# Score tiles leave PSUM in two instructions instead of three: one over 768 columns in two banks, one over 384

## The chip, the cores and the metric

The kernel runs on one core of a Trainium2 chip. The metric is the device time of one execution in microseconds, from the median of several runs. A core has TensorE (PE in the profile; its weight loads are PEld), VectorE (DVE), ScalarE (ACT), GpSimd (POOL) and SyncE (SP). TensorE writes its results to PSUM, which this kernel uses as eight banks of 512 fp32 columns on 128 partitions; VectorE and ScalarE carry them from there to SBUF.

## The reference

```python
# attention: batch 4, 8 heads, 1152 keys, head_dim 64; neighbouring queries are averaged: 576 queries
q_pool = q.reshape(B, H, S // 2, 2, D).mean(axis=3)
scores = scale * np.matmul(q_pool, k.transpose(0, 1, 3, 2))
scores = scores - np.max(scores, axis=-1, keepdims=True)
attn = np.exp(scores)
attn = attn / (np.sum(attn, axis=-1, keepdims=True) + 1e-09)
attn_out = np.matmul(attn, v)
...
# then, on x of (4, 576, 512):
mixed = np.real(fft(fft(x, axis=1), axis=2))
u = x + mixed
un = (u - mean(u)) / np.sqrt(var(u) + 1e-06)
out = u + np.maximum(un @ w_ch1, 0.0) @ w_ch2      # w_ch1 512 x 2048, w_ch2 2048 x 512, kept as float64
```

## The kernel before

The 32 heads are worked in 16 pairs. A pair has five units: for query blocks 0 to 3 a unit holds two score tiles, one of each head of the pair, of 128 queries by 1152 keys; the last unit holds one tile in which the last 64 queries of both heads are stacked. While the tiles of one unit are turned and multiplied by the values, the scores of the next unit are computed, so each pass of the loop in `attention` issues on TensorE, in this order: score pieces of the next unit, the product with the values of the unit before (`av`, L263), groups of transposes of this unit (`t_step`, L247), with more score pieces between the groups.

A score tile is made in three pieces of 384 columns (`s_piece`, L220 and L222). Each piece is two accumulating matmuls into one bank (four in the stacked tile), and one VectorE instruction that scales it, stores it to SBUF (`sp`) and keeps the smallest value of each row in a column of `bia`; the second and third piece take the column of the piece before as an operand, so the last column holds the smallest value of the row. The eviction is recorded as two instructions, the pass itself and a short read of the accumulator. When all pieces of a tile are out, ScalarE takes the exponential over the 1152 columns in place (`s_exp`, L234). In the next pass the tile is turned, four blocks of 128 columns to a group, and each group is copied from PSUM to `pt`, by ScalarE except for the fourth group of a two-tile unit, which VectorE copies (L250).

Below, the two tiles of a unit are A and B, their pieces A0, A1, A2, B0, B1, B2, and the five groups of transposes g0 to g3 (four blocks each) and gc (the last block of both tiles). A pass of the kernel before then runs on TensorE: A0, A1, `av`, g0, A2, B0, g1, B1, B2, g2, g3, gc. A mark as in A0' means the same step in the next pass.

PSUM is split into three pools: `ps_t`, five banks, for all score pieces and most transposes; `ps_o`, one, for `av`; `ps_f`, two, for the dense layers. While the first four pairs run, no dense layer runs yet, and four of five groups of transposes go to `ps_f` (by a counter, `steps`). A pool hands out its banks in turn, so an allocation waits until what was written to the same bank as many allocations ago as the pool has banks has been read out.

Between the steps of a pass the generator yields an estimate of its TensorE time, and a planner (`background`, `credit`, `due`) puts in the other work: blocks of the dense layers (`ffn`, twelve matmuls into one bank, L685 to L687, then ScalarE L704 and VectorE L705, or VectorE L717), the Fourier transform and the normalisation of a finished batch (`dft`, `norm`, mostly chains of VectorE instructions), the conversion of the weights from float64 (`convert`, ScalarE, VectorE and GpSimd), and the reciprocal of the row sums (`den_recip`: VectorE L271 and L272, then a transpose on TensorE at L276). Instructions on each engine run in the order in which they are written out this way. After the last unit (`tail`) the dense layers of the last batches use all banks of `ps_t` and `ps_f`, chosen by the counter `turn`.

## Time and profile before

| | |
|---|---|
| median of 3 runs | 1044.74 us (1042.09 to 1045.94) |
| the profiled execution: its own time | 1044.25 us |
| its span, first to last instruction | 1042.5 us |
| mean granted TensorE clock over the span | 0.981 |
| TensorE busy | 975.8 us, 94% of the span |
| VectorE busy | 605.4 us, 58% |
| ScalarE busy | 523.7 us, 50% |
| score evictions on VectorE (L222) | 432, of 384 columns each |

The span is 1.75 us shorter than the execution's own time. Busy time of TensorE counts pipelined matmuls until their modelled end, so where it is 100% the engine is without a gap, but not at its peak. The clock is a share of 2.4 GHz: 0.5 would be 1.2 GHz throughout. A row of waits names who stood idle, behind the arrow what ended the idle time, then the total, how often, and the longest.

### The profile page before, as it was taken

How to read it: one execution, taken by the hardware profiler on the slowest of the kernel's cores; microseconds unless marked ns; L12 is line 12 of the kernel's file. 1: busy time of each engine (PE TensorE's matmuls, PEld its weight loads, DVE VectorE, ACT ScalarE, POOL GpSimd, SP SyncE). 2: the span in 40 equal slices, each digit the busy share in tenths (PEclk: the TensorE clock that was granted, in tenths of full speed). 3: DMA queues.
4: the chain of work that ended last, by engine and by line, in shares of the span. 5: the costliest groups of instructions: out<-in, count | busy, mean ns of one | idle time of the engine just before them, and what ended most of it. 6: DMA issues, size and time to landing. Idle time of an engine off the chain costs nothing.

```text
span 1042.5 us, 19731 instructions
## 1 busy us (share of the span) xinstructions
PE 975.8 (94%) x7392; PEld 847.5 (81%) x7392; DVE 605.4 (58%) x1518; ACT 523.7 (50%) x1017; POOL 421.7 (40%) x609
## 2 busy tenths in 40 slices
PE   6999988898998899899999999999999989999998
PEld 4898977777877777687788888787788867899998
DVE  5556868889754687787644475666544245522222
ACT  5778877767745566466444554554444231201100
POOL 3555678788386575996323141633200010000000
PEclk9999999999999899999999999999999989999999
DMA  6545467646566856475745464163532334733443
GB/s 186 170 135 180 135 197 239 183 127 221 143 203 243 276 181 220 140 240 187 217 145 179 135 193 129 33 207 109 170 104 102 115 120 126 230 134 122 126 136 122
DMA packets 62515, 170.91 MB, mean 164 GB/s; under 512 B 16770, under 2 KB 20242, under 8 KB 62420
## 3 DMA queue, kind: packets, MB, share of 16 engines
q1 hardware_dynamic: 58100, 151.96, 46.1%
q0 software_dynamic: 4320, 17.70, 5.3%
q8 instruction: 58, 0.95, 0.4%
q14 instruction: 37, 0.30, 0.1%
HBM read 146.88 MB, written 22.75 MB: 163 GB/s over the span
## 4 chain that ended last, share of the span: by engine, by line
PE 50%; DVE 5%; POOL 3%; ACT 2%; DMA 2%; issue 1%; SPq 0%; DVEq 0%; ACTq 0%; POOLq 0%
PE f L685 7%; PE f L687 6%; PE f L686 6%; PE s L220 6%; PE o L263 5%; PE t L247 5%; PE t L685 4%; PE t L687 4%; PE t L686 4%; DVE sp L222 1%; DMA out<-x 1%; PE f L505 1%; DMA w<-w 1%; POOL wb L646 1%; POOL rest L646 0%
## 5 line engine op out<-in xcount | busy, mean ns | idle before, releaser
L222 DVE TENSOR_SCALAR_CACHE_REDUCE sp<-s,bia 128x384 f32<-128x384 f32 x288 | 177.2, 615 | 79.2 <-PE s L220 57.2
L220 PE MATMUL s<-ks,qh 128*128 128x384 f32 x480 | 185.7, 387 | 19.8 <-ACT qh L164 6.4
L234 ACT ACTIVATE sp<-sp,bia 128x1152 f32<-128x1152 f32 x144 | 180.2, 1256 | 1.8 <-DVE sp L222 1.6
L263 PE MATMUL o<-pt,vs 128*64 128x128 f32 (+1 forms) x2880 | 171.7, 273 | 9.4 <-DVE pt L250 5.0
L263 PEld LDWEIGHTS o<-pt,vs 128*64 128x64 f32 x2880 | 151.5, 141 | 33.6 <-issue 20.7
L250 ACT COPY pt<-t 128x512 f32<-128x512 f32 (+2 forms) x243 | 124.5, 527 | 91.3 <-PE t L247 90.2
L220 PE MATMUL s<-ks,ql 128*128 128x384 f32 x480 | 164.9, 344 | 0.4 <-POOL ql L165 0.4
L247 PE MATMUL t<-ident,sp 128*128 128x128 f32 x1045 | 150.6, 276 | 7.1 <-DVE sp L222 3.7
L247 PEld LDWEIGHTS t<-ident,sp 128*128 128x128 f32 x1045 | 121.5, 141 | 28.3 <-DVE sp L222 6.7
L220 PEld LDWEIGHTS s<-ks,qh 128*128 128x128 f32 x480 | 92.4, 193 | 31.7 <-ACT pt L250 9.0
L189 POOL TENSOR_TENSOR ks<-kr,ks 64x288 fp32r<-64x288 f32 x120 | 103.4, 894 | 29.7 <-issue 12.6
L705 DVE SCALAR_TENSOR_TENSOR g<-f,g 128x512 fp32r<-128x512 f32 (+1 forms) x52 | 34.7, 667 | 110.0 <-ACT g L704 110.0
L220 PEld LDWEIGHTS s<-ks,ql 128*128 128x128 f32 x480 | 93.1, 194 | 1.1 <-POOL ql L165 0.8
L704 ACT ACTIVATE g<-f 128x512 fp32r<-128x512 f32 (+1 forms) x52 | 30.1, 579 | 119.7 <-PE f L687 119.7
L186 POOL TENSOR_TENSOR qr<-qr 128x288 f32<-128x288 f32 x60 | 49.9, 850 | 92.6 <-DMA qr<-in_q 92.6
L197 POOL TENSOR_TENSOR ql<-qr,qh 128x288 fp32r<-128x288 f32 (+2 forms) x75 | 55.7, 768 | 75.0 <-ACT qh L194 73.7
L685 PE MATMUL f<-unh,w 128*128 128x512 f32 (+1 forms) x208 | 82.8, 398 | 2.7 <-DMA w<-w 2.7
L646 POOL TENSOR_TENSOR rest<-rest,wa 128x256 f32<-128x256 f32 x64 | 48.2, 770 | 89.2 <-DVE wa L639 64.0
L222 DVE TENSOR_SCALAR_CACHE_REDUCE sp<-s 128x384 f32<-128x384 f32 x144 | 78.4, 545 | 6.1 <-PE s L220 4.4
L687 PE MATMUL f<-unl,w 128*128 128x512 f32 (+1 forms) x208 | 80.4, 387 | 0.0
L686 PE MATMUL f<-unh,w 128*128 128x512 f32 (+1 forms) x208 | 80.2, 386 | 0.0
L685 PE MATMUL f<-g,w 128*128 128x512 f32 (+1 forms) x188 | 74.2, 394 | 1.9 <-DVE g L705 0.9
(149 smaller groups left out, 1761.3 us busy)
## 6 DMA issues: line engine op xcount, KB each, us to landing
w<-w SPq DMA_DIRECT2D x128, 512.0 KB
qr<-in_q SPq DMA_DIRECT2D x30, 576.0 KB
ks<-in_k POOLq DMA_DIRECT2D x30, 576.0 KB, 6.1
wraw<-in_w SPq DMA_DIRECT2D x32, 512.0 KB
w<-wraw SPq DMA_DIRECT2D x32, 512.0 KB
vs<-in_v SPq DMA_DIRECT2D x32, 288.0 KB
kr<-in_k SPq DMA_DIRECT2D x30, 288.0 KB
out<-x SPq DMA_DIRECT2D x12, 256.0 KB
```

The costliest lines, as they stand in the source:

```text
L189: nc.gpsimd.tensor_tensor(ks[D:, c], kr[D:, c], ks[D:, c].bitcast(F32), op=ALU.subtract)
L197: nc.gpsimd.tensor_tensor(ql[:, z], qr[:, 0, x:y], qh[:, z].bitcast(F32), op=ALU.subtract)
L220: nc.tensor.matmul(ps, lhsT=l, rhs=k, start=i == 0, stop=i == len(ops) - 1)
L222: nc.vector.tensor_scalar(sp[n, j][:, c], ps, -0.0625, bt[:, pc - 1:pc] if pc else None, op0=ALU.mult, op1=ALU.min, accum_out=bt[:, pc:pc ...
L234: last_exp[0] = nc.scalar.activation(t, t, AF.Exp, bias=bia.pop((n, j))[:, 2:3], scale=-1.0, accum_out=den[pr][:, col:col + 1]).ins
L247: nc.tensor.transpose(ps[:, i * P:i * P + P], sp[k][:, c * P:(c + 1) * P], ident)
L250: (nc.vector.tensor_copy if eng == "v" else nc.scalar.copy)(pt[:, :o], ps[:, :o])
L263: nc.tensor.matmul(po[y * D:y * D + D, :w], lhsT=qkv[2 * pr + y][3][:, c, :], rhs=pt[:, o:o + w], start=c == 0, stop=c == NKC - 1)
L646: nc.gpsimd.tensor_tensor(o[:, c], x[:, c], y[:, c], op=op)
L685: nc.tensor.matmul(ps, lhsT=ah, rhs=bh, start=first, stop=False)
L686: nc.tensor.matmul(ps, lhsT=al, rhs=bh, start=False, stop=False)
L687: nc.tensor.matmul(ps, lhsT=ah, rhs=bl, start=False, stop=last)
```

## The change

Each score tile leaves PSUM in two instructions. The first two pieces become one: four matmuls (two for each half) into a tile of two neighbouring banks, and one eviction over 2 x 384 columns. The third piece stays as it was, in a bank of `ps_t`. Two of the five banks of `ps_t` become the new pool `ps_s`, which holds one such wide tile; `ps_t` keeps three. Where a pass issued two pieces it now issues one (wide, small, wide, small), and the last small piece stands between g2 and g3. A wide piece is called A0 or B0 from here on and a small one A1 or B1, so a pass is: A0, `av`, g0, A1, g1, B0, g2, B1, g3, gc. In the first four pairs two of five groups of transposes go to `ps_t` instead of one, and in the tail the dense layers turn through five banks instead of seven, since `ps_s` isn't used there.

```diff
--- before.py
+++ after.py
@@ -72,7 +72,8 @@
     xp = pool("x", XB)
     scr = pool("scr", 2, space=bass.MemoryType.DRAM)
     scw = pool("scw", 1, space=bass.MemoryType.DRAM)
-    ps_t = pool("ps_t", 5, space=PSUM)
+    ps_t = pool("ps_t", 3, space=PSUM)
+    ps_s = pool("ps_s", 1, space=PSUM)
     ps_o = pool("ps_o", 1, space=PSUM)
     ps_f = pool("ps_f", 2, space=PSUM)
 
@@ -95,7 +96,7 @@
     def gtile():
 
         turn[0] += 1
-        if tail[0] and turn[0] % 7 < 5:
+        if tail[0] and turn[0] % 5 < 3:
             return ps_t.tile([P, 512], F32, tag="t", name="t")
         return ps_f.tile([P, 512], F32, tag="f", name="f")
 
@@ -209,21 +210,27 @@
     def s_piece(n, j, pc):
         if pc == 0:
             sp[n, j] = spp.tile([P, S], F32, tag="sp", name="sp")
-            bia[n, j] = smp.tile([P, 3], F32, tag="bia", name="bia", bufs=6)
-        ps = ps_t.tile([P, 512], F32, tag="t", name="s")[:, :384]
-        c = slice(pc * 384, pc * 384 + 384)
+            bia[n, j] = smp.tile([P, 2], F32, tag="bia", name="bia", bufs=6)
+        if pc == 0:
+            ps = ps_s.tile([P, 2, 512], F32, tag="s", name="s")[:, :, :384]
+        else:
+            ps = ps_t.tile([P, 1, 512], F32, tag="t", name="s")[:, :, :384]
+        n_c = 2 - pc
         ops = []
         for m in (n, n + 1) if j == 4 else (n,):
             ks, qh, ql, _ = qkv[m]
-            ops += [(t[:, j * P:j * P + P], ks[:, c]) for t in (qh, ql)]
-        for i, (l, k) in enumerate(ops):
-            nc.tensor.matmul(ps, lhsT=l, rhs=k, start=i == 0, stop=i == len(ops) - 1)
+            ops += [(t[:, j * P:j * P + P], ks) for t in (qh, ql)]
+        for x in range(n_c):
+            c = slice((2 * pc + x) * 384, (2 * pc + x) * 384 + 384)
+            for i, (l, k) in enumerate(ops):
+                nc.tensor.matmul(ps[:, x], lhsT=l, rhs=k[:, c], start=i == 0, stop=i == len(ops) - 1)
         bt = bia[n, j]
+        c = slice(pc * 768, pc * 768 + n_c * 384)
         nc.vector.tensor_scalar(
-            sp[n, j][:, c], ps, -0.0625, bt[:, pc - 1:pc] if pc else None,
+            sp[n, j][:, c].rearrange("p (a b) -> p a b", a=n_c), ps, -0.0625, bt[:, 0:1] if pc else None,
             op0=ALU.mult, op1=ALU.min, accum_out=bt[:, pc:pc + 1],
         )
-        return 740 if j == 4 else 390
+        return (740 if j == 4 else 390) * n_c
 
     def s_exp(n, j):
         pr = n // 2
@@ -231,7 +238,7 @@
             den[pr] = smp.tile([P, 9], F32, tag="den", name="den", bufs=3)
         t = sp[n, j]
         col = 5 * (n % 2) + j
-        last_exp[0] = nc.scalar.activation(t, t, AF.Exp, bias=bia.pop((n, j))[:, 2:3], scale=-1.0,
+        last_exp[0] = nc.scalar.activation(t, t, AF.Exp, bias=bia.pop((n, j))[:, 1:2], scale=-1.0,
                                            accum_out=den[pr][:, col:col + 1]).ins
 
     steps = [0]
@@ -239,7 +246,7 @@
     def t_step(pr, items, eng):
 
         steps[0] += 1
-        if pr < 4 and steps[0] % 5 != 2:
+        if pr < 4 and steps[0] % 5 not in (2, 4):
             ps = ps_f.tile([P, 512], F32, tag="f", name="f")
         else:
             ps = ps_t.tile([P, 512], F32, tag="t", name="t")
@@ -329,11 +336,12 @@
         for _ in parts(0):
             pass
         for pc, _ in enumerate(parts(1)):
-            s_piece(0, 0, pc)
+            if pc < 2:
+                s_piece(0, 0, pc)
         for _, q_part, _, _, _ in first:
             q_part(*Q0[1])
         s_exp(0, 0)
-        for pc in range(3):
+        for pc in range(2):
             s_piece(1, 0, pc)
         s_exp(1, 0)
         nc.sync.dma_start(onesm, cst[4, :, P:2 * P])
@@ -354,7 +362,7 @@
                 if j in (1, 3):
                     prep_head(2 * pr + 2 + j // 2)
             nxt = unit_tiles(*units[i + 1]) if i + 1 < len(units) else []
-            pieces = deque((n, jj, pc) for n, jj in nxt for pc in range(3))
+            pieces = deque((n, jj, pc) for n, jj in nxt for pc in range(2))
             expd = []
 
             def some(k):
@@ -363,7 +371,7 @@
                     if pieces:
                         p = pieces.popleft()
                         pe += s_piece(*p)
-                        if p[2] == 2:
+                        if p[2] == 1:
                             expd.append(p[:2])
                 return pe
 
@@ -390,15 +398,17 @@
             else:
                 k = tiles[0]
                 g = [[(k, c, [(0, 0), (1, D)]) for c in cs] for cs in (range(4), range(4, 8), range(8, 9))]
-            yield some(2)
+            yield some(1)
             if held:
                 yield finish(*held)
             yield tr(g[0], "a")
-            yield some(2)
+            yield some(1)
             yield tr(g[1], "a")
-            yield some(2)
+            yield some(1)
             for y, x in enumerate(g[2:]):
                 yield tr(x, "v" if j < 4 and y == 1 else "a")
+                if y == 0:
+                    yield some(1)
             exps()
             if j == 4:
                 after(1500, den_recip(pr))
```

## Rows read from the trace of the kernel before

**Rows 1.** The page's first part: busy time, share of the span, instructions, by engine.
```profile
PE 975.8 (94%) x7392; PEld 847.5 (81%) x7392; DVE 605.4 (58%) x1518; ACT 523.7 (50%) x1017; POOL 421.7 (40%) x609
```

**Rows 2.** Windows by stage: length, busy (xcount) by engine, granted clock, DMA.
```profile
20.00:130.00 110.00, 106.83 (x1118) 96.77 (x1117) 72.07 (x224) 85.98 (x170) 62.10 (x98) 1.00 0.53 160
130.00:520.00 390.00, 351.22 (x2789) 294.83 (x2788) 286.69 (x683) 244.95 (x473) 272.74 (x376) 0.96 0.63 201
520.00:820.00 300.00, 293.77 (x2312) 251.80 (x2310) 155.99 (x407) 147.78 (x288) 74.75 (x111) 1.00 0.42 133
820.00:1042.50 222.50, 212.78 (x1151) 196.53 (x1149) 80.29 (x178) 35.86 (x70) 5.67 (x8) 0.98 0.46 142
```

**Rows 3.** TensorE's waits, 130 to 520 us: total us, times, longest us.
```profile
PE t L276 <- DVE den L272: 5.2, 6, 1.5
PE o L263 <- DVE pt L250: 5.0, 4, 2.8
PE o L263 <- ACT pt L250: 4.1, 2, 3.9
PE s L220 <- DVE sp L222: 3.9, 5, 2.2
PE s L220 <- ACT pt L250: 3.7, 4, 1.7
PE t L247 <- DVE sp L222: 3.3, 3, 2.1
PE t L247 <- ACT pt L250: 3.0, 2, 2.5
...
PE f L247 <- ACT pt L250: 2.5, 2, 2.1
```

**Rows 4.** TensorE's waits, 20 to 130 us: all that is listed.
```profile
PE f L247 <- ACT pt L250: 3.2, 8, 1.2
```

**Rows 5.** VectorE's groups by shape: the evictions of score pieces (busy, mean ns).
```profile
L222 DVE TENSOR_SCALAR_CACHE_REDUCE sp<-s,bia 128x384 f32<-128x384 f32 x288 | 177.2, 615 | 79.2 <-PE s L220 57.2 <-DVE sp L222 0.5
L222 DVE TENSOR_SCALAR_CACHE_REDUCE sp<-s 128x384 f32<-128x384 f32 x144 | 78.4, 545 | 6.1 <-PE s L220 4.4 <-ACT pt L250 1.5
```

**Rows 6.** VectorE's timeline, one unit near 58 us: start, duration.
```profile
58.14 0.55 DVE L222 TENSOR_SCALAR_CACHE_REDUCE sp<-s 128x384 f32<-128x384 f32 x1
...
58.82 0.62 DVE L222 TENSOR_SCALAR_CACHE_REDUCE sp<-s,bia 128x384 f32<-128x384 f32 x1
...
59.57 0.62 DVE L222 TENSOR_SCALAR_CACHE_REDUCE sp<-s,bia 128x384 f32<-128x384 f32 x1
...
60.11 0.68 DVE L250 COPY pt<-t 128x512 f32<-128x512 f32 x1
```

**Rows 7.** TensorE's timeline in the same unit.
```profile
58.10 0.42 PE L220 MATMUL s<-ks,qh 128*128 128x384 f32 x1
...
58.53 0.34 PE L220 MATMUL s<-ks,qh 128*128 128x384 f32 x1
...
58.89 0.60 PE L247 MATMUL f<-ident,sp 128*128 128x128 f32 x4
59.32 0.60 PE L247 MATMUL t<-ident,sp 128*128 128x128 f32 x4
59.76 0.38 PE L247 MATMUL f<-ident,sp 128*128 128x128 f32 x2
59.90 0.42 PE L220 MATMUL s<-ks,qh 128*128 128x384 f32 x1
```

**Rows 8.** ScalarE's timeline in the same unit.
```profile
58.44 0.59 ACT L250 COPY pt<-f 128x512 f32<-128x512 f32 x1 [0.45 <-PE f L247]
59.58 0.97 ACT L250 COPY pt<-f 128x512 f32<-128x512 f32 x2 [0.55 <-PE f L247]
```

**Rows 9.** TensorE's timeline: a wait near 432 us.
```profile
432.52 0.44 PE L220 MATMUL s<-ks,qh 128*128 128x384 f32 x1 [2.22 <-DVE sp L222]
```

**Rows 10.** Windows around a shorter wait near 299 us and that one.
```profile
295.00:310.00 15.00, 13.28 (x99) 11.14 (x97) 10.17 (x23) 8.27 (x18) 14.03 (x21) 1.00 0.49 164
425.00:440.00 15.00, 12.47 (x84) 9.17 (x82) 13.46 (x30) 6.03 (x11) 13.89 (x20) 0.89 0.31 112
```

## The prediction

> **What bounds the kernel now.** I read the busy times first: TensorE is busy 94% of the span, no other engine above 58% except its own weight loads [rows 1]. So what the change takes off VectorE is worth only what TensorE waits for VectorE. Next the windows by stage [rows 2]: TensorE stands idle 3.2 us from 20 to 130 us (the first pairs, no dense layers), 38.8 us from 130 to 520 (390 minus 351.2; conversions, transforms and dense layers run beside the attention), 6.2 us from 520 to 820, and 9.7 us behind that, when no score tile is left. The middle stretch decides. VectorE is busy 73.5% of it (286.7 of 390), 52% of the stretch behind.
>
> The waits of that stretch say what ended the idle time [rows 3]. VectorE ends 17.4 us in 18 waits: 5.2 for the reciprocals, 5.0 for the copy of g3, 3.9 and 3.3 for score evictions that hold a bank. ScalarE's copies to `pt` end 13.3 us (4.1, 3.7, 3.0, 2.5). In the first stretch the whole list is one row: transposes that wait in `ps_f` for ScalarE, 3.2 us [rows 4].
>
> A long wait costs more than itself. The wait of 2.22 us at 432.5 us ended on a score eviction [rows 9]; the windows around it have a granted clock of 0.89, those around a wait of 1.7 us (the longest of that row of [rows 3]) have 1.00 [rows 10]. An 0.11 share of 15 us is 1.65 us of TensorE time lost, as if 3.3 us ran at 1.2 instead of 2.4 GHz. That it was the wait that lowered the clock is a reading from these two, not shown.
>
> **What VectorE saves.** In a clean unit its evictions start 0.68, 0.75 and 0.54 us apart [rows 6]: 1.97 us a tile. Their mean lengths are 545 ns without and 615 ns with the operand from the piece before [rows 5]. The wide eviction is in no row. The copy of 512 columns takes 0.68 [rows 6] and the eviction of 384 takes 0.545, so a column is worth about 1.05 ns, and 384 more columns about 0.40 us: the wide one lasts 0.95, and the next starts 1.08 behind its start (0.68 + 0.40). A tile then holds VectorE for 1.08 + 0.54 = 1.62 us, 0.35 less, a two-tile unit 0.70 less, all 144 tiles 50 us. The bounds: if two banks in one instruction cost as much as two instructions (2 x 0.545 = 1.09 long), 0.21 a tile is left; if the columns are all that counts and a column costs less, 0.40. I take 0.35. The matmuls are as many as before, and so are their loads; ScalarE's work is the same.
>
> **What that is worth on TensorE.** First, the 18 waits on VectorE can shrink by at most 0.70 each, 12.6 us, when each follows a unit whose evictions are queued ahead of it. But some are shorter than 0.70, and a TensorE that comes earlier meets the same chain of the transform or the conversion earlier. I take half, 6.3 us (bounds 0 and 12.6). Second, the banks: a group of transposes waited for an eviction (A2, B0) to free its bank, 3.3 us in three waits. Now transposes take the bank of an earlier transpose, or of a small piece long evicted; this lies within the 6.3. Third, the clock: the two longest waits on score evictions, 2.2 and 2.1 us, would come down to about 1.5, below the 1.7 that left the clock at 1.00. I count 2 x 1.65 = 3.3 us (bounds 0 and 5).
>
> **What the first pairs gain.** Before, g2, g3 and gc often fall to the two banks of `ps_f` in a row, and gc waits for ScalarE's copy of g2. With two of five groups in `ps_t` (steps 2 and 4), gc follows an allocation two or three groups back in each of the four pairs, by the counter's phase. I take 4 of the 5.7 us (3.2 and 2.5) [rows 3, 4]; bounds 1 and 5.7.
>
> **What three banks cost.** From the fifth pair on, `ps_t` serves g0, A1, g1, g2, B1, g3, gc, and each allocation waits for the third before it. For most steps the work between is as long as before. One is new: gc waits for g2, with only B1 and g3 between. In the clean unit g2 starts at 58.89, g3 takes 0.44, a small piece 0.36 (58.53 to 58.89) [rows 7]; so gc wants to start 0.43 + 0.36 + 0.44 = 1.23 us behind g2's start. ScalarE starts the copy of g2 0.69 behind that start (59.58) and copies for 0.59 [rows 8]: 1.28. So gc is 0.05 to 0.1 late in a unit where the planner puts nothing between, when ScalarE is prompt, and as late as ScalarE is when it isn't. The cap is the work that TensorE could have done before `av` needs the same copy: gc 0.14 and A0' some 0.8, about 0.9 us, and what the planner puts between. Twelve pairs with three such units (in the fourth no small piece stands there) are 36. At 0.1 each that is 3.6 us. For the 18 of the crowded stretch I add as much again and a little, 0.12 each, since ScalarE is late there at times (its 13.3 us): 2.2, together 5.8 us (bounds 0 and 36 x 0.9 = 32).
>
> **What the single wide buffer costs.** A0' waits until B0 is evicted. Between are g2 0.43, B1 0.36, g3 0.44, gc 0.14 [rows 7]: 1.37 us. Against it stand 1.08 of VectorE and the way from TensorE to the reader, 0.26 as ScalarE shows it (59.32 to 59.58): 1.34. Any foreign instruction ahead of it on VectorE makes A0' late, and behind A0' stands `av` in TensorE's queue; but before the change VectorE had five pieces to finish by then (3.40 us), now three instructions (2.70). I take 1.5 us in all (bounds 0 and 15). The copy of g3 on VectorE comes behind B1, nearer to `av`, which reads it from its ninth matmul on; that is in the half that I left out above. The planner's estimates per pass add up to the same, `s_exp` and the startup keep their order. In the tail five banks instead of seven turn under blocks of twelve matmuls, at 0.18 us each (212.8 over 1151 [rows 2]) 2.2 us a block. Its eviction is hidden by the four blocks that follow before the bank is used again, 8.9 us, so I cost it at nothing; without that cover the tail would show waits on L704 and L705.
>
> The sum goes against the profiled execution: 1044.25 - 4 - 6.3 - 3.3 + 5.8 + 1.5 = 1037.95, so 1038 us. That execution lies 0.5 below the median of the runs, within their spread of 3.9.
>
> The Trainium skill (Perfetto Trace Analysis, section Optimizing Scalar/DVE Operations) says that larger operations help where the engine is saturated, and that where it isn't, but leaves gaps on others, smaller ones may complete sooner. The 73.5% and 52% here lie below saturation, so by that rule the fourth way below would decide and the sum would be its 1051; by the rows it is 1038. The 17.4 us for which TensorE waits on VectorE [rows 3] are gaps that a late queue left, not a long instruction, and so the rows bear the first half of the rule out rather than the second.
>
> **The rivals.**
> 1. No gain beyond the first pairs: TensorE meets the same late transform, reciprocal and ScalarE copies a little earlier, and new short waits at gc take the rest. For it: ScalarE's 13.3 us are nearly as large as VectorE's 17.4, and the change doesn't touch them. Then 1044.25 - 4 - 3 + 5.8 + 1.5 = 1044.5.
> 2. Slower through gc behind g2: the same place as above, but ScalarE (63% busy in the crowded stretch, 245 of 390) is late as a rule. At 0.55 us in each of 36 units it costs 20, and against all gains: 1044.25 - 13.6 + 20 + 1.5 = 1052. It decides from a mean of 12.1/36 = 0.34 us on. Against it: the clean unit shows 0.05.
> 3. The wide eviction is no cheaper (0.21 or less saved): the 6.3 and 3.3 become 3.8 and 1.6, and the time 1042. If two banks read at half pace, the wide one lasts 0.8 longer (768 x 1.05 ns), A0' waits that long in each of 64 two-tile units, 51 us, and the time is above 1090.
> 4. Slower through the wide buffer: B0's results come later by the two matmuls (0.36) and 0.40 of eviction, and where a foreign instruction as long as the copy of g3, 0.68 [rows 6], stands ahead on VectorE, A0' waits for most of that. In one of three of 64 units that is 64/3 x 0.65 = 14 us in place of the 1.5, with the gains halved (6.8 of 13.6): 1044.25 - 6.8 + 5.8 + 14 = 1057; at one in five, 8 us, 1051. With whole gains it decides from 7.8 us on (13.6 - 5.8). Against it: VectorE has 0.70 us less ahead of A0' in just these units.
>
> **How the numbers follow.** Chances: forecast 0.50 (1028 to 1041), rival 1 0.28 (1041 to 1046), rival 2 0.10, rival 4 0.08, rival 3 0.04. About 0.5% (5.2 us) is what a measurement of this kernel can tell from no change, so faster means below 1039.5. Of the forecast 0.42 lie there; its rest 0.08, rival 1 and 0.03 of the others are within 0.5%: 0.39; the rest, 0.19, is slower. The likeliest case gives 1038. With all gains full and no cost the sum is 1044 - 5.7 - 12.6 - 5 = 1021, which needs everything at once; I put the lower end at 1028. The upper end reaches to rivals 2 and 4 without their larger forms: 1051. Outside are some 0.2: half of rivals 2 and 4, all of rival 3's slow form, and the forecast's own low tail.
>
> **What would show it.** Score evictions should be 288, the wide ones about 0.95 us, and VectorE's busy time some 40 us lower (one eviction of 0.615 and its read fewer, 0.40 more, per tile, 144 times). The wait row of the first stretch should shrink to near nothing. From 130 to 520 us the rows of transposes waiting for L222 should be gone, those for reciprocals and g3 shorter. gc should show waits of about 0.1 us on L250, many of them, and the clock of that stretch should rise above 0.96. The forecast is wrong if the waits on L250 grow by more than 10 us in total, if A0' waits for L222 more than the 3.9 us of before, or if the waits on VectorE stay as long as they are with 50 us less in its queue.

## The result and the profile after

The changed kernel takes 1055.62 us (median of 9 runs, 1052.58 to 1060.35) beside 1043.81 us for the kernel before (9 runs, 1038.68 to 1051.54): a ratio of 1.0112, interval 1.0082 to 1.0143. It is slower, by about 12 us, where 1038 was predicted, with 1051 as the upper end. The profiled execution took 1055.62, its span is 1053.9 us at a mean granted clock of 0.979 (before 1042.5 and 0.981).

The busy times of the changed kernel, from the first part of its page:

```profile
PE 974.9 (93%) x7392; PEld 848.3 (80%) x7392; DVE 567.1 (54%) x1230; ACT 527.0 (50%) x1017; POOL 420.7 (40%) x609
```

VectorE has 38 us less to do than in [rows 1], as planned; TensorE does the same work and the span is 11.4 us longer. Where TensorE stands idle is in the windows by stage (columns as in [rows 2]):

```profile
core 0: us, PE busy (x) PEld busy (x) DVE busy (x) ACT busy (x) POOL busy (x), PEclk, DMA share, GB/s
20.00:130.00 110.00, 107.00 (x1120) 97.15 (x1119) 67.16 (x162) 86.43 (x169) 64.08 (x101) 1.00 0.54 166
130.00:520.00 390.00, 342.10 (x2742) 288.36 (x2742) 264.05 (x548) 241.91 (x467) 267.02 (x368) 0.96 0.62 197
520.00:820.00 300.00, 296.84 (x2305) 252.79 (x2302) 144.45 (x319) 150.15 (x288) 77.63 (x117) 1.00 0.44 139
820.00:1053.90 233.90, 218.84 (x1207) 202.36 (x1205) 81.44 (x180) 38.95 (x76) 5.67 (x8) 0.97 0.43 133
```

Idle is the length less PE busy: 3.0 us in the first pairs (3.2 before), 47.9 in the crowded stretch (38.8), 3.2 behind it (6.2), 15.1 in the last (9.7). The crowded stretch lost 9.1 us though VectorE is busy 22.6 us less in it. Its waits, to be laid beside [rows 3]:

```profile
engine line waited for: us in total, times, longest us
PE t L254 <- ACT pt L257: 8.4, 8, 2.4
PE s L226 <- DVE sp L229: 7.3, 9, 1.3
PE o L270 <- ACT pt L257: 5.7, 1, 5.7
PE o L270 <- DVE pt L257: 4.4, 2, 3.0
PE f L695 <- DMA w<-w: 4.0, 2, 2.1
PE f L507 <- ACT y L508: 3.4, 2, 1.8
PE f L548 <- DVE lsum L541: 2.9, 1, 2.9
```

The waits for the reciprocals (5.2 us before) are gone. In their place transposes wait for ScalarE's copies, score pieces for VectorE's evictions, and one `av` stands 5.7 us. All rows together that name VectorE as what ended the wait come to 18.5 us in 18 waits in this stretch, against 18.7 in 21 before.

The span is best cut where the last `av` ends. Two windows of the kernel before, split there, and two of the kernel after:

```profile
0.00:821.60 821.60, 764.42 (x6280) 652.15 (x6280) 525.90 (x1343) 488.79 (x950) 416.06 (x601) 0.98 0.54 170
821.60:1042.50 220.90, 211.36 (x1115) 195.32 (x1113) 79.47 (x175) 34.92 (x67) 5.67 (x8) 0.98 0.46 141
```

```profile
0.00:831.70 831.70, 767.31 (x6304) 655.37 (x6304) 488.53 (x1057) 493.33 (x952) 415.07 (x601) 0.98 0.54 169
831.70:1053.90 222.20, 207.62 (x1091) 192.89 (x1089) 78.53 (x173) 33.65 (x65) 5.67 (x8) 0.97 0.44 136
```

The attention ends 10.1 us later: 7.2 us more idle time (64.4 against 57.2) and 2.9 more busy. TensorE has issued 24 instructions more by then (6304 against 6280) and 24 fewer behind it: two blocks of the dense layers, twelve matmuls each, which the planner now puts in front of the attention's end (912 matmuls of the dense layers by the program's order, against 888). Yet the rest isn't shorter for it, 222.2 us against 220.9: its idle time grew from 9.5 to 14.6 us, about what the two blocks take. The waits of the rest, of the kernel after and then of the kernel before:

```profile
PE t L507 <- DVE xs L483: 5.0, 1, 5.0
PE t L695 <- ACT unh L606: 4.0, 1, 4.0
PE f L588 <- DVE dg L578: 1.5, 1, 1.5
```

```profile
PE t L497 <- DVE xs L473: 4.4, 1, 4.4
PE f L685 <- DMA w<-w: 0.4, 1, 0.4
PE t L687 <- DMA unl<-left: 0.4, 1, 0.4
PE t L685 <- DMA w<-w: 0.3, 1, 0.3
```

After the change TensorE runs out of dense blocks there and waits 4.0 us for `unh`, the normalised input of the last batch; the kernel before has no such row. In these traces the end of the kernel depends on the last batch's chain of transform and normalisation, so two blocks taken out of it shortened nothing.

### The profile page after: what moved, and what is told of

Same layout as the page of the kernel before. It is cut to its first block, busy times and chain, and to the rows that moved or that the text cites. A ratio compares the mean times of both kernels' runs of the same rounds, so it can differ in the third digit from the quotient of the medians.

```text
span 1053.9 us, 19278 instructions
## 1 busy us (share of the span) xinstructions
PE 974.9 (93%) x7392; PEld 848.3 (80%) x7392; DVE 567.1 (54%) x1230; ACT 527.0 (50%) x1017; POOL 420.7 (40%) x609
## 4 chain that ended last, share of the span: by engine, by line
PE 53%; DVE 4%; DMA 3%; POOL 3%; ACT 2%; issue 2%; SPq 0%; DVEq 0%; ACTq 0%; POOLq 0%
PE f L695 7%; PE f L697 7%; PE f L696 7%; PE o L270 6%; PE s L226 6%; PE t L254 6%; PE t L695 4%; PE t L696 4%; PE t L697 4%; DMA w<-wraw 2%; PE f L515 1%; DVE sp L229 1%; POOL wb L656 1%; POOL wraw L656 1%; PE f L507 1%
## 5 line engine op out<-in xcount | busy, mean ns | idle before, releaser
L226 PE MATMUL s<-ks,qh 128*128 128x384 f32 x480 | 189.3, 394 | 21.8 <-DVE sp L229 12.7
L257 ACT COPY pt<-t 128x512 f32<-128x512 f32 (+2 forms) x257 | 132.6, 526 | 116.2 <-PE t L254 115.0
L254 PE MATMUL t<-ident,sp 128*128 128x128 f32 x1106 | 172.4, 280 | 13.3 <-ACT pt L257 9.5
L270 PE MATMUL o<-pt,vs 128*64 128x128 f32 (+1 forms) x2880 | 166.5, 269 | 10.5 <-ACT pt L257 5.9
L270 PEld LDWEIGHTS o<-pt,vs 128*64 128x64 f32 x2880 | 146.8, 139 | 33.7 <-issue 20.9
L254 PEld LDWEIGHTS t<-ident,sp 128*128 128x128 f32 x1106 | 132.9, 143 | 39.4 <-ACT pt L257 17.0
L229 DVE TENSOR_SCALAR_CACHE_REDUCE sp<-s 128x768 f32<-128x768 f32 x144 | 136.6, 948 | 36.4 <-PE s L226 32.9
L229 DVE TENSOR_SCALAR_CACHE_REDUCE sp<-s,bia 128x384 f32<-128x384 f32 x144 | 88.3, 613 | 76.0 <-PE s L226 71.6
L714 ACT ACTIVATE g<-f 128x512 fp32r<-128x512 f32 (+1 forms) x56 | 32.1, 574 | 137.0 <-PE f L697 137.0
L695 PE MATMUL f<-unh,w 128*128 128x512 f32 (+1 forms) x224 | 89.4, 399 | 4.0 <-DMA w<-w 4.0
L697 PE MATMUL f<-unl,w 128*128 128x512 f32 (+1 forms) x224 | 86.6, 387 | 0.0
L696 PE MATMUL f<-unh,w 128*128 128x512 f32 (+1 forms) x224 | 86.5, 386 | 0.0
L695 PE MATMUL f<-g,w 128*128 128x512 f32 (+1 forms) x204 | 78.8, 386 | 1.5 <-issue 1.5
L697 PE MATMUL f<-g,w 128*128 128x512 f32 (+1 forms) x204 | 77.3, 379 | 0.0
```

What stands on the lines that cost most here:

```text
L226: nc.tensor.matmul(ps[:, x], lhsT=l, rhs=k[:, c], start=i == 0, stop=i == len(ops) - 1)
L229: nc.vector.tensor_scalar(sp[n, j][:, c].rearrange("p (a b) -> p a b", a=n_c), ps, -0.0625, bt[:, 0:1] if pc else None, op0=ALU.mult, op1= ...
L254: nc.tensor.transpose(ps[:, i * P:i * P + P], sp[k][:, c * P:(c + 1) * P], ident)
L257: (nc.vector.tensor_copy if eng == "v" else nc.scalar.copy)(pt[:, :o], ps[:, :o])
L270: nc.tensor.matmul(po[y * D:y * D + D, :w], lhsT=qkv[2 * pr + y][3][:, c, :], rhs=pt[:, o:o + w], start=c == 0, stop=c == NKC - 1)
L695: nc.tensor.matmul(ps, lhsT=ah, rhs=bh, start=first, stop=False)
```

## The experiments

All ratios are of times against the kernel before, measured beside it, with 95% intervals in brackets. Where two ratios are compared, the uncertainty given is the root of the sum of the squares of their half widths. The experiments ran in five groups (e1 to e4, e5 to e8, e9 to e12, e13 to e16, e17 and e18); the median of the kernel before was 1042.0 to 1043.1 us beside four of them, and 1046.3 beside e5 to e8. A comparison of one of these four with a run of another group is therefore less sure than the uncertainty says. "Steps" below are the places in a pass where `attention` yields to the planner, and the time that it tells it there: before, 780 ns of scores behind g0; after, 390 there and 390 behind g2, with one yield more (in a pass whose next unit has two tiles). The sum of a pass is the same. The kernel before and e2 have the "old" steps, the changed kernel and e1 the "new" ones. Of each edit the main lines are shown; `...` stands where others are left out.

**e1: the order and the steps alone** (three evictions and five banks stay).

```diff
             yield tr(g[0], "a")
-            yield some(2)
+            yield some(1)
             yield tr(g[1], "a")
             yield some(2)
             for y, x in enumerate(g[2:]):
                 yield tr(x, "v" if j < 4 and y == 1 else "a")
+                if y == 0:
+                    yield some(1)
```

> Three pieces of 384 columns and five banks as before the change, but issued in the changed kernel's order (A0 A1, av, g0, A2, g1, B0 B1, g2, B2, g3, gc), with its steps to the planner, which puts 24 more dense matmuls ahead of the end of the attention (912 in place of 888). Theory plan (the planner's grid of steps moved the filler and the chain of the transform, and the tail runs short of cover): 1051 to 1058, near the changed kernel. Theory banks (gc waits for g2 in three banks) and theory wide (A0' waits for the one wide buffer): 1040 to 1047, near the kernel before, since neither is in it.

Measured 1.0091 [1.0057, 1.0126]. No bank and no eviction is changed here, and a loss of nearly the whole size is there.

**e2: the changed kernel, the planner told the old steps.** The matmuls stand in the new order; only what is yielded differs.

```diff
             yield tr(g[0], "a")
-            yield some(1)
+            yield some(1) + (390 if len(nxt) == 2 else 0)
...
-                yield tr(x, "v" if j < 4 and y == 1 else "a")
+                pe = tr(x, "v" if j < 4 and y == 1 else "a")
                 if y == 0:
-                    yield some(1)
+                    some(1)
+                yield pe
```

> The changed kernel with its two instructions and its banks, but the planner is told the same estimates at the same steps as before the change, so that all filler stands where it stood (888 dense matmuls ahead of the end of the attention). Theory plan: 1036 to 1046. Theories banks and wide: 1052 to 1058, no better than the changed kernel.

Measured 1.0066 [1.0039, 1.0093]; against the changed kernel 0.46% less, give or take 0.41. The old steps give back part, not all.

**e3: the changed kernel with the wide piece evicted in two instructions** (`ps_s` holds two tiles of one bank).

```diff
-    ps_s = pool("ps_s", 1, space=PSUM)
+    ps_s = pool("ps_s", 2, space=PSUM)
...
```

> The changed kernel's order, planner steps and three banks, but the two banks of ps_s are two tiles of one bank, each evicted by its own instruction of 384 columns. Theory wide: the wait of A0' goes, 1047 to 1051. Theory banks and theory plan: 1055 to 1061, since VectorE gets its 40 us back and nothing else changes.

Measured 1.0173 [1.0141, 1.0204]: on the new steps the wide instruction is worth 0.6% (give or take 0.44), and three banks instead of five cost 0.8% (e3 against e1, give or take 0.46). "Three banks" stands here for all that goes with the split of the five: two banks for the first two pieces of a tile alone, three for the rest, the first pairs' and the tail's share of them.

**e4: the changed kernel with gc in `ps_f` from the fifth pair on.**

```diff
-        if pr < 4 and steps[0] % 5 not in (2, 4):
+        if (pr < 4 and steps[0] % 5 not in (2, 4)) or (pr >= 4 and len(items) < 4):
```

> The changed kernel, but from the fifth pair on the last, short group of transposes of a unit takes a bank of ps_f, so it doesn't wait for the copy of g2. Theory banks: the waits of transposes on ScalarE's copies fall by most of their 9.5 us, 1046 to 1051. Theories plan and wide: 1054 to 1058.

Measured 1.0092 [1.0064, 1.012]: 0.2% less than the changed kernel, within the intervals, though the row of transposes in `ps_t` that wait for ScalarE's copies fell from 9.5 us to 1.7. The row of score pieces waiting for VectorE rose from 12.7 to 15.5.

**e5: e1 on the old steps**, by the edit of e2.

> The order-alone kernel (three evictions, five banks, the changed order of pieces), but the planner is told the estimates of the kernel before, so filler stands where it stood. If the order-alone kernel was slow by the planner (24 dense matmuls, 5.4 us, moved out of a tail that doesn't get shorter): 1042 to 1048. If it was slow by the place of the pieces themselves: 1050 to 1055.

Measured 0.9956 [0.9924, 0.9987]. The new order of the pieces by itself gains a little, if anything: this is one of the four beside a slower kernel before, and its median, 1041.74 us, lies just below the 1042.0 to 1043.1 of the other groups. e1 and e5 differ only by the steps: 1.35% (give or take 0.47) by the ratios, 11.6 us or 1.1% by the medians.

**e6 and e7: `av` ahead of A0'**, so that no `av` stands behind a late A0'. e6 does it in e2, e7 in the kernel before as a control.

```diff
-            yield some(1)
             if held:
-                yield finish(*held)
+                yield 780 if len(nxt) == 2 else 1480 if nxt else 0
+                pe = finish(*held)
+                some(1)
+                yield pe
...
```

> The changed kernel on the old plan (e2), with A0 issued behind av instead of ahead of it, so that the wide buffer has some 2 us more to be evicted. Theory wide: the 13.0 us for which A0 waited for evictions in e2 go, less what av now waits for the copies of g2 and gc: 1040 to 1047. Theory banks: no change or slower, 1049 to 1056, since av meets ScalarE's copies earlier.

> The control: the kernel before the change, with A0 and A1 behind av. There A0 waits for evictions only 2.0 us, and av waits 9.3 us for copies. Theory wide: 1043 to 1050, no gain or a small loss, so that a gain of e6 is one on the wide buffer. If it gains as e6 does, the order of av is a thing of its own.

Measured e6 1.0097 [1.0063, 1.0131], e7 1.0177 [1.0134, 1.0221]. In e6 the row of score pieces waiting for VectorE fell from 15.4 us (e2) to 3.0 over the whole span, and a row that is 3.2 us in e2 heads the list instead:

```profile
PE o L270 <- DVE pt L257: 13.1, 13, 3.1
...
PE s L226 <- DVE sp L229: 3.0, 3, 2.2
```

The queue in order had only been reordered: `av` now comes to VectorE's copy of g3 before it is done. The control missed its forecast: the same edit costs the kernel before 1.8%, with 19.7 us of this wait. So e6 doesn't tell what the wait of A0' is worth by itself; it loses only 0.3% on e2 (give or take 0.43), and what it may have won is hidden in what the edit costs.

**e8: e2 with gc in `ps_f`** (the edit of e4).

> The changed kernel on the old plan (e2), with the short group of transposes in a bank of ps_f from the fifth pair on. Theory banks: 1043 to 1047. Theory wide: 1047 to 1052, since gc waits only 3.3 us in e2 and A0 13.0.

Measured 0.9996 [0.9962, 1.003], 0.7% below e2 (give or take 0.43; 0.5% by the medians). With the old steps and gc out of the three banks the loss is gone, in this one run; the same edit gained 0.2% in e4 and nothing in e11. The traces don't show what it won: they are of executions only 1 us apart (1048.0 and 1047.0), gc's own waits fall from 3.3 to 1.2 us, and those of score pieces for VectorE rise from 15.4 to 17.4.

**e9: e3 on the old steps.**

> The split kernel (three evictions, three banks, ps_s as two single banks) on the old plan. Beside the order-alone kernel on the old plan (e5, ratio 0.996) it has only the banks changed, and beside e2 (1.007) only the wide instruction undone. If three banks cost what they cost on the new plan (0.8%): 1.004 times before. If the wide instruction gains what it gained there (0.6%): 1.013 times before. The two can't both hold with the sums of the new plan unless the plan and the banks add to one another.

Measured 1.0053 [1.0022, 1.0084]. Against e5 the three banks cost 0.97% (give or take 0.44); against e2 the wide instruction gains nothing (0.13% the other way, give or take 0.41).

**e10 and e11: B0 earlier**, pieces in the order A0, B0, A1, B1, in e2 (e10) and in e8 (e11), so that more lies between B0 and A0'.

```diff
-            pieces = deque((n, jj, pc) for n, jj in nxt for pc in range(2))
+            pieces = deque((n, jj, pc) for pc in range(2) for n, jj in nxt)
...
             yield tr(g[1], "a")
-            yield some(1)
+            yield some(1) + (390 if len(nxt) == 2 else 0)
...
```

> e2 with the wide piece B0 between g0 and g1 and the small A1 between g1 and g2, so that B0 is evicted one group of transposes and a small piece earlier ahead of A0'. Theory wide: most of the 13.0 us of A0's waits go, and the ratio falls from 1.007 to between 0.995 and 1.000. Theory banks: 1.005 to 1.010, since gc still waits for g2 in three banks.

> e10 with the short group of transposes in a bank of ps_f. If the wide buffer and the banks are two costs of their own, the gains add: 0.988 to 0.994 times before. If they are one queue that moves its wait about: as e8 or e10, 0.996 to 1.003.

Measured 1.0072 [1.0044, 1.0101] and 1.008 [1.005, 1.0111]; e11 is 0.84% slower than e8 (give or take 0.46). Two rows from the waits of e2 and two from those of e10, both over the whole span:

```profile
PE s L226 <- DVE sp L229: 15.4, 18, 2.3
...
PE t L254 <- ACT pt L257: 5.9, 9, 1.6
```

```profile
PE t L254 <- ACT pt L257: 14.3, 18, 3.6
...
PE s L226 <- DVE sp L229: 3.3, 3, 2.4
```

12.1 us of waiting for VectorE went, 8.4 us of waiting for ScalarE came, and the time stayed.

**e12: the kernel before, the steps alone.** No instruction is changed; the planner is told the changed kernel's steps.

```diff
+            two = len(nxt) == 2
             yield tr(g[0], "a")
-            yield some(2)
+            yield some(2) - (390 if two else 0)
             yield tr(g[1], "a")
             yield some(2)
             for y, x in enumerate(g[2:]):
                 yield tr(x, "v" if j < 4 and y == 1 else "a")
+                if y == 0:
+                    yield 390 if two else 0
```

> The kernel before the change, its pieces, order and banks untouched; only the estimates that it yields to the planner stand at the changed kernel's steps (780, 1950, 420, 390, 420, 780, 420, 390, 420, 210), so that 912 dense matmuls come ahead of the end of the attention. Theory plan: 1.006 to 1.015 times before, that is 1050 to 1059. If the plan is nothing by itself: 0.997 to 1.003.

Measured 1.0113 [1.0079, 1.0147], as much as the whole change. Its windows, split where the last `av` ends:

```profile
0.00:833.30 833.30, 771.44 (x6304) 659.33 (x6305) 515.80 (x1345) 491.16 (x952) 413.46 (x601) 0.98 0.54 169
833.30:1053.40 220.10, 206.45 (x1089) 191.88 (x1089) 78.50 (x173) 33.60 (x65) 5.66 (x8) 0.98 0.45 137
```

Again 24 instructions more in front (6304), 61.9 us idle instead of 57.2, and a rest that is no shorter.

**e13 and e14: these steps in half of the pairs**, the first seven (e13, `two = len(nxt) == 2 and pr < 7`) or the last nine (e14, `pr >= 7`).

> The kernel before with the new steps to the planner in the first seven pairs only. 36 dense matmuls come earlier by the end of the seventh pair (60 for 24), and 24 by the end of the attention (912 for 888). If the loss is laid down there: 1.008 to 1.014 times before, all of e12's. If it comes from the later steps: 0.998 to 1.003.

> The kernel before with the new steps to the planner from the eighth pair on only; 888 dense matmuls ahead of the end of the attention, as before. If the loss is laid down in the first seven pairs: 0.997 to 1.003 times before. Otherwise 1.006 to 1.014.

Measured 1.001 [0.9983, 1.0037] and 1.0001 [0.9967, 1.0036]. Neither half carries the loss, nor do they add up to it: 912 matmuls stand in front in e13, 888 in e14, and neither has the long tenth pair of which the next section tells (65.9 and 63.4 us).

**e15 and e16: the 24 matmuls by another way.** A higher rate in the kernel before (0.90, shown; 912 in front), and a lower one in e5 (0.80 in the same place; 864 in front).

```diff
-    RATES = [0.0, 0.98, 0.85, 0.85, 0.85]
+    RATES = [0.0, 0.98, 0.85, 0.90, 0.85]
```

> The kernel before with its own steps, but with a rate of 0.90 in place of 0.85 for the dense layers' credit while the third batch of the attention is done and before the fourth: the placement is the same up to the thirteenth pair, and 912 dense matmuls come ahead of the end. If the tail is bound by its chain and doesn't shorten by the 5.4 us moved out of it: 1.004 to 1.007 times before. If the tail takes its share: 0.998 to 1.002.

> e5, the fastest so far, with a rate of 0.80 in that place: 864 dense matmuls ahead of the end, 24 more left to the tail. If the tail is bound by its chain and has room for them: 0.988 to 0.993 times before. If it has none left: 0.994 to 0.999, as e5.

e15 (0.90) measured 1.0043 [1.0007, 1.0079], e16 (0.80) 1.001 [0.9979, 1.0042]. In e15 the rest takes 220.0 us, with 2.6 us of waiting for `unh`; in e16 it grows to 226.5, and e16 is 0.54% above e5 (give or take 0.45, and of another group). So, as far as this noise lets one tell, 888 is about the point from which the rest gets no shorter with more in front, and longer with less.

**e17 and e18: a load of a weight block planned longer ahead of its conversion**, in the changed kernel and in the kernel before. This takes away the 5.7 us wait of `av`, which hung on such a load.

```diff
         nc.sync.dma_start(w, src[f].bitcast(I32).rearrange("p (c x) -> p c x", x=2))
-        yield 4000 if going else 7000
+        yield 7000 if going else 7000
```

> The changed kernel, but a conversion's first ScalarE instruction is planned 7000 in place of 4000 behind its load while dense layers run; 60 and 912 dense matmuls come ahead of the ends of the seventh and the last pair, as in the changed kernel. If ScalarE's wait for that load makes the long tenth pair: the pair falls from 80 to some 70 us, and the ratio from 1.011 to 1.002 to 1.006. If the pair is long by the crowd as a whole: 1.008 to 1.014.

> The control: the same edit on the kernel before the change. ScalarE waits for such loads there too (6.5 us near 359 us), so a gain of up to 0.4% may be had here as well: 0.996 to 1.001. Only what e17 gains beyond this is of the tenth pair.

Measured e17 1.0108 [1.0069, 1.0148], e18 0.9947 [0.9918, 0.9976]. In e17 the wait is gone and the tenth pair 8.7 us shorter, but others came, such as this one in the same pair, from its waits between 420 and 500 us:

```profile
PE f L568 <- DVE sq L563: 3.8, 1, 3.8
```

e18, at 1036.97 us, is the fastest version run, ahead of both kernels; e5 is next. The two together were not run.

## Why the prediction was wrong

**The step that failed.** "The planner's estimates per pass add up to the same, `s_exp` and the startup keep their order." From this the changed steps were costed at nothing. The sum is the same, but not where in the pass the planner is called and what it is told there. e12 changes only that and costs 1.13%, the size of the whole result; e1 against e5 gives 1.35% for the same difference; taken back in the changed kernel itself, the steps give 0.46% (e2, give or take 0.41). So a term put at nothing is 5 to 14 us, by what else is changed.

It is not the whole miss. With the old steps the change still measures 1.0066, where the sum of the prediction is 0.994 (1037.95 of 1044.25). There **other terms were mis-sized**: three banks cost 8.6 to 10.1 us where 5.8 had been put down, the first pairs gave none of their 4, and the gain of the wide instruction on TensorE, 8.1 us with the wait of its single buffer taken off, was 6.4 us on the new steps and nothing on the old. The premise of that gain was that "the 18 waits on VectorE can shrink by at most 0.70 each". VectorE's queue did get shorter, but in the crowded stretch the waits that it ends are 18.5 us after, 18.7 before. That they would "stay as long as they are with 50 us less in its queue" was named as a sign that the forecast is wrong.

That the time lies where rivals 2 and 4 put it (1052, and 1051 to 1057) is a coincidence. gc's waits come to 8.8 us, not to rival 2's 20; those of A0' come to 7.5, near the 8 of rival 4's smaller form, but for another reason than the one it gave; and neither counts the steps.

The path from the kernel before to the changed one, one part at a time:

```
                              on the new steps        on the old steps
order of pieces                                       -0.44%  (e5)
steps                         +1.35%  (e5 to e1)
three banks instead of five   +0.82%  (e1 to e3)      +0.97%  (e5 to e9)
one wide instruction          -0.61%  (e3 to after)   +0.13%  (e9 to e2)
all                            1.0112                  1.0066
```

Each difference is uncertain by 0.4 to 0.5%, and those with e5 by more, since its group had the slower kernel before. The parts don't simply add: the wide instruction gains on the new steps and not on the old ones.

**How the steps cost it: one part likely, one open.** Shown: with the new steps throughout, two blocks more of the dense layers come in front of the attention's end, and the rest, which waits for the last batch, gives nothing back for them. At the rest's rate (220.9 us for 3 x 344 matmuls of the dense layers and some small ones) 24 take at most 5.1 us. That they cost this much is likely and not shown: e15 moves the 24 by the rate alone and costs 0.43% (4.5 us), but e13, with 912 in front too, costs 0.10%, and the two are not told apart (0.33%, give or take 0.45). Open: what the rest of the 1.1 to 1.35% is. These are the lengths of the tenth pair and the end of the attention, taken from the traces, with the matmuls of the dense layers in front of that end:

```
            before  after   e1    e12    e3  |  e2    e5    e9    e15   e13   e14   e18   e17
tenth pair    66.4   79.7  77.7  79.2  79.8 | 65.5  65.3  66.5  66.5  65.9  63.4  62.1  71.0
end          821.6  831.7 826.5 833.3 842.6 | 825.7 817.7 827.2 823.4 820.2 817.6 813.2 830.5
in front       888    912   912   912   912 |  888   888   888   912   912   888   888   912
```

With the new steps throughout, the tenth pair is 11 to 13 us longer (without the edit of e17). That is not by itself the loss: it holds 72 matmuls of the dense layers instead of 60, and the pairs beside it are shorter, in the kernel after the ninth 65.5 us for 70.9 (84 such matmuls for 108) and the eleventh 55.6 for 61.0 (108 in both). The three together take 200.8 us for 198.3, with 12 such matmuls fewer (264 for 276). Still, in the kernel after one sees what happens in the tenth. ScalarE's timeline there, start and length, with the idle time before an instruction in brackets:

```profile
463.39 0.60 ACT L714 ACTIVATE g<-f 128x512 fp32r<-128x512 f32 x1 [1.86 <-PE f L697]
463.89 0.61 ACT L653 CAST wraw<-wb 128x512 fp32r<-128x512 f32 x1
472.04 0.66 ACT L636 ACTIVATE wa<-wraw 128x512 f32<-128x512 f32 x1 [7.54 <-DMA wraw<-in_w]
472.60 0.36 ACT L257 COPY pt<-t 128x256 f32<-128x256 f32 x1
```

and TensorE's:

```profile
465.74 1.59 PE L270 MATMUL o<-pt,vs 128*64 128x128 f32 x26
473.01 0.69 PE L270 MATMUL o<-pt,vs 128*64 128x128 f32 x4 [5.69 <-ACT pt L257]
```

and those of SP, which issues the transfers:

```profile
460.75 0.33 SPq L662 DMA_DIRECT2D w<-wraw  x1
468.21 0.33 SPq L627 DMA_DIRECT2D wraw<-in_w  x1
```

ScalarE stands 7.54 us before a step of a conversion whose load lands at about 472.0; the load was issued only at 468.21, behind the landing of an earlier conversion's store. The copy of gc stands behind it in ScalarE's queue and `av` waits 5.69 us for that copy. The windows around it:

```profile
455.00:466.00 11.00, 11.00 (x70) 9.54 (x72) 8.86 (x20) 5.71 (x9) 7.38 (x10) 1.00 0.98 311
467.00:482.00 15.00, 9.31 (x54) 7.54 (x50) 4.56 (x12) 7.15 (x15) 9.20 (x16) 0.77 0.53 178
482.00:499.00 17.00, 14.01 (x128) 11.57 (x126) 10.32 (x27) 11.16 (x19) 7.89 (x13) 1.00 0.42 130
```

The granted clock is 0.77 in the window that holds this wait, so part of it ran at 1.2 GHz. But this wait alone is not the cause: e17 takes it away and gains nothing in all (1.0108), and e13 and e14, each with half of the steps, have no long tenth pair. What the runs leave is that the place of each conversion, transform and dense block in the queues follows from the steps, and that different placements lie about 1% apart; which meeting of queues makes the difference stays open. One more thing goes with the steps: over the runs of each kernel the mean granted clock, as a share of 2.4 GHz, has a median of 0.9755 to 0.9775 in the five with the new steps throughout (after, e1, e3, e4, e12) and of 0.981 to 0.983 in the kernel before beside them; in e2, e5, e8 and e9, with the old steps, it is 0.981 to 0.9845. On 1050 us 0.005 is an estimated 5 us. No run tells whether this is a cause or follows from the longer waits. The match is not strict: e17, as slow as the changed kernel, has 0.980, and e11 and e15, with the old steps, have 0.979 and 0.9785.

**VectorE's saving: right.** The wide eviction takes 948 ns (0.95 predicted), 144 times, and VectorE's busy time fell by 38 us (some 40 predicted). Two rows of the changed kernel's groups by shape, beside [rows 5]:

```profile
L229 DVE TENSOR_SCALAR_CACHE_REDUCE sp<-s 128x768 f32<-128x768 f32 x144 | 136.6, 948 | 36.4 <-PE s L226 32.9 <-PE t L254 1.6 <-PE f L254 1.2
L229 DVE TENSOR_SCALAR_CACHE_REDUCE sp<-s,bia 128x384 f32<-128x384 f32 x144 | 88.3, 613 | 76.0 <-PE s L226 71.6 <-PE f L254 0.5
```

**What it is worth on TensorE: 9.6 us predicted with the clock (6.3 and 3.3), less 1.5 for the single wide buffer; 6.4 us measured on the new steps** (0.61%, e3 to after, give or take 0.44), **and nothing on the old** (e9 to e2, 0.13% the other way, give or take 0.41). On the new steps that fits, within the noise; on the old it doesn't. The reciprocals' 5.2 us of waits did go. That the freed time would return as waits on the next releaser was rival 1's mechanism, and e10 shows it. The clock of the crowded stretch stayed at 0.96, so the 3.3 us put down for it didn't come.

**The first pairs: no gain, 4 us predicted.** The waits from 20 to 130 us after, beside [rows 4]:

```profile
PE s L226 <- DVE sp L229: 2.0, 3, 0.7
PE f L254 <- ACT pt L257: 1.0, 1, 1.0
```

The wait for `ps_f` fell from 3.2 to 1.0, and A0' put 2.0 in its place.

**Three banks: too small, and the mechanism right only in part.** 5.8 us were predicted; 0.8 and 1.0% are 8.6 and 10.1 us. Counted step by step in the traces, gc waits for ScalarE's copies 8.8 us after, 2.3 before, and not in many waits of 0.1 us but in few long ones: all transposes in `ps_t` wait for such copies 9.5 us in 11 waits, the longest 2.4. That is the mechanism of the prediction, on the new steps (8.6 us in e3, 1.4 in e1). But all waits that ScalarE's copies to `pt` end grew only from 18.2 to 20.8 us over the span, since others shrank. And on the old steps gc waits no longer with three banks than with five (3.8 us in e9, 3.9 in e5, for either engine); there score pieces wait for ScalarE's copies instead, in e5 and in e9:

```profile
PE s L220 <- ACT pt L250: 2.4, 5, 0.7
```

```profile
PE s L228 <- ACT pt L257: 8.1, 5, 2.6
```

Taking gc alone out of the three banks gained 0.7% once (e8) and nothing clear of noise twice (e4, e11).

**The single wide buffer: too small, by a pass that was overlooked.** 1.5 us were predicted for A0'; in units of two tiles it waits for the eviction 7.5 us after, against 2.0 before, and 13.0 in e2. "If A0' waits for L222 more than the 3.9 us of before" was named as what would show the forecast wrong, and it did. The prediction counted g2, B1, g3 and gc, 1.37 us, between B0 and A0'. In the pass in which a pair's stacked tile is turned, g2 and g3 don't exist: only its one last block and B1 stand there. 7.1 of the 7.5 us fall on the A0' behind this pass, 10.6 of the 13.0 in e2. TensorE there, in the kernel after, and VectorE's eviction of B0:

```profile
45.98 0.27 PE L254 MATMUL f<-ident,sp 128*128 128x128 f32 x1
46.01 0.42 PE L226 MATMUL s<-ks,qh 128*128 128x384 f32 x1
46.27 0.34 PE L226 MATMUL s<-ks,ql 128*128 128x384 f32 x1
47.29 0.45 PE L226 MATMUL s<-ks,qh 128*128 128x384 f32 x1 [0.69 <-DVE sp L229]
```

```profile
46.27 0.96 DVE L229 TENSOR_SCALAR_CACHE_REDUCE sp<-s 128x768 f32<-128x768 f32 x1 [0.60 <-PE f L254]
47.16 0.08 DVE L229 DVE_READ_ACCUMULATOR sp<-s 128x1 f32 x1
```

Rival 4 had a foreign instruction ahead of the eviction on VectorE; here there is none, VectorE was idle for 0.60 us before it. What this wait costs in time no run isolates: e10 takes it away and gains nothing, since another takes its place, and in e6 the edit has a cost of its own. An order in which only the pass of the stacked tile is changed was not run.

**The tail: right.** With five banks instead of seven its waits, shown above, hold none for L714 or the evictions behind it.

**The rule of the Trainium skill** (Perfetto Trace Analysis, section Optimizing Scalar/DVE Operations), that where VectorE isn't saturated but leaves gaps on other engines smaller instructions may let work complete sooner, agrees in direction with A0', which waits 7.5 us behind evictions of 948 ns where it waited 2.0 before; the runs do not bear it out in the time, where splitting the wide eviction gains nothing measurable on the old steps and loses 0.6% on the new.

## What to carry to other kernels

Where a planner fills the gaps of a main loop, what the loop tells it, and where, is part of the kernel's schedule: when an edit moves those points, first run the old kernel with nothing but the points moved, and the new kernel with the old ones. A bank taken away is priced by the engine that must release it at its latest, and in the shortest pass of the loop, not in a clean unit. And a wait that is removed from a queue in order counts as a gain only when the next releaser in line has been looked at too: four of these edits (e4, e6, e10, e17) removed the wait they aimed at, and none gained clear of noise.

## What the runs showed of the hardware that was not expected

One VectorE instruction over 2 x 384 columns in two PSUM banks took 948 ns against 545 for 384 columns in one [rows 5]: 1.05 ns for each further column, as much as the prediction had estimated for a column from rows of one bank. No extra cost of the second bank shows.
